# Two PSUM accumulators with alternating sums, and tensor-by-scalar products on GpSimd, in a convolution and feed-forward kernel

## The chip, the core and the metric

The kernel runs on one core of a Trainium2 chip. The metric is the device time of one execution in microseconds (us), lower being better. Three executions of the kernel before took 510.12, 510.33 and 511.39 us (median 510.33).

The engines are called as the profile calls them: PE (TensorE) multiplies matrices and writes its results into PSUM, DVE (VectorE), ACT (ScalarE) and POOL (GpSimd) work on tiles, and SP (SyncE) sends DMAs. POOL sends DMAs too.

## The reference

```python
# x: (8, 3904, 192), weight: (8 heads, 7 taps); 8 heads of 24 channels
w = softmax(weight, axis=-1)
x_pad = np.concatenate([np.zeros((B, 6, D)), x], axis=1)
out[b, s, h*24:(h+1)*24] = sum over k of w[h, k] * x_pad[b, s + k, h*24:(h+1)*24]
x = out.reshape(31232, 192)
a = x @ w1                      # 192 x 1024
b = x @ w2                      # 192 x 1024
return ((a * b) @ w3) @ w_out   # 1024 x 1024, 1024 x 192
```

A causal convolution of 7 taps, one set of taps to each head, goes along each of the 8 sequences of 3904 rows. Its output goes into two products with 192 x 1024 weights, the elementwise product of the two follows, and then the two weights at the end, which the kernel multiplies into one of 1024 x 192 (`W_sb`) beforehand.

## The kernel before, in words

**Rows and rounds.** The 31232 rows are halved into two streams of 15616 (`NS = 2`, index r). A round R is 512 consecutive rows of both streams (`CH = 512`); there are 31, the last one with 256 rows. The channels go in three pieces of 64 (`NP = 3`, index k); a tile of 128 partitions holds one such piece of both streams.

**First product** (`first_product`, L618 to L651). For each round and each of the eight 128-column blocks ft of the weights, PE makes `pa` (with w1) and `pb` (with w2), six matmuls of 512 columns each, three channel pieces by two streams, the two streams on the two halves of the array's rows. ACT copies `pa` to `asb` in bf16 (L640), and DVE multiplies `asb` by `pb` into `abT` (L643). `pa` and `pb` take one PSUM quarter each.

**Second product** (`second_product`, L678 to L703; `half_rows` in four later phases). For a round and a stream, PE multiplies `abT` by `W_sb` into one quarter `ops` in 32 matmuls of 192 columns, ACT copies it to `osb` (L690), and SP sends it out.

**Quarters.** All of PSUM is four buffers of 128 x 2 x 512 fp32 (two banks each), one pool tag that is handed round in turn (`banks`, L104). Whatever PE writes takes the next of the four, and waits until the last reader of what was in it is done.

**Phases.** Three rounds at a time make a phase p, counted from 0: the first products of its rounds (24 steps of `pa` and `pb`), then the second products of the same rounds (six, one for each round and stream). In phases 0, 2 and 5 matmuls of the convolution stand between the second products (`places`, `convolve`). The fourth and fifth phase are p = 3 and p = 4, and hold none.

**Where the convolution is done.** For most rows by PE, as products with a band matrix. For the rounds in `SIDE` it is done elsewhere, by *tasks*: one channel piece of two rounds each. Rows are cast to bf16 in HBM by DMAs of the POOL queue (`side_cast`, L506), transposed into a `raw` tile by DMAs of the SP queue (`side_transpose`, L515), ACT makes the first of seven terms into an fp32 accumulator (`side_first`, L520), and DVE adds the six others, one SCALAR_TENSOR_TENSOR each: raw x tap + accumulator (`side_sums`, L538). The last of them writes bf16 into `side`, which a later phase's first products read. There are two accumulators in SBUF, `acc_of[0]` and `acc_of[1]`, taken in turn by tasks. A planner (L797 to L816) fills phases with sums by a room of 12 sums a phase, so two whole tasks, one after the other, in p = 3 (tasks 5 and 6) and in p = 4 (tasks 7 and 8). `side_steps` (L821) issues them between the second products: an entry with a number (`at`) is a task's first term on ACT, due after so many second products; sums follow in the list's order up to the next first term that isn't issued yet.

**What POOL does beside this.** Half tasks (`POOL_AT`), 512 rows each, by a product into `tmp` (L584, TENSOR_TENSOR with a tap broadcast over the row) and an addition (L596, last one L591). In phases 3 to 6 POOL has two half tasks each, issued at the start of the first products, and behind them a one-element copy `pace` (L948) that holds the DMAs of the POOL queue until a given step of the first products is done.

Of the kernel before, what the change touches and what calls it, by code (L numbers as in the profile page):

```python
# [8 lines left out]
FP32 = mybir.dt.float32  # L9
BF16 = mybir.dt.bfloat16  # L10
AX = mybir.AxisListType
ALU = mybir.AluOpType
# [4 lines left out]
def kernel(  # L17
# [10 lines left out]
    nc = tc.nc  # L28

    B, S, D = x.shape  # L30
    H, K = weight.shape
# [5 lines left out]
    NS = 2  # L37
    TS = B * S // NS
    CH = 512
# [34 lines left out]
    t0 = (LAG + 3) * CH  # L74
# [25 lines left out]
    psum = ctx.enter_context(tc.tile_pool(name="psum", bufs=4, space=bass.MemoryType.PSUM))  # L100
    dram = ctx.enter_context(tc.tile_pool(name="dram", bufs=1, space=bass.MemoryType.DRAM))
    ctx.enter_context(tc.manual_schedule())

    def banks(name):  # L104
        return psum.tile([128, NS, CH], FP32, tag="banks", name=name)

    def banks_bf16(name):
        return psum.tile([128, 16, 128], BF16, tag="banks", name=name)

    def slot(shape, dtype, name):  # L110
        return stage.tile(shape, dtype, tag="slot", bufs=6, name=name)
# [76 lines left out]
    for r in range(NS):  # L188
        p = group(r, 0).start
# [12 lines left out]
        out=diag, in_=diag, pattern=[[-1, 128 + 8]], compare_op=ALU.is_equal,  # L202
# [11 lines left out]
    for i in range(4):  # L214
        d = diag[i * C:i * C + C, i * C + 2 * i:i * C + 2 * i + C]
        nc.vector.tensor_copy(
            out=cmask[i * C:i * C + C],
# [62 lines left out]
    for i in range(4):  # L280
# [16 lines left out]
        op=ALU.mult)  # L297
    for r, w0, w1, f in ((0, 0, HW, A), (1, HW // 2, HW, A), (1, 0, HW // 2, V)):
        f(out=xb_of[0][0][0][group(r, 0), w0:w1, :], in_=begin[group(r, 0), w0:w1, :])
    p = group(1, 0).start  # L300
# [177 lines left out]
    for q in SIDE:  # L478
        for k in range(NP):
            left = [h for h in range(2) if (q, k, h) not in BY_POOL]  # L480
            if left:
                tasks.append((q, k, half_of(q, left[0])[0], half_of(q, left[-1])[1]))
    side_of, acc_of, raw_of, cast_to = {}, [], [], set()
    RAW = HALO + 2 * CH

    def side_tiles():
# [31 lines left out]
    def side_first(i):  # L518
        p, k, t0, t1 = tasks[i]
        nc.scalar.activation(  # L520
            out=acc_of[i % 2][:, 0:t1 - t0], in_=raw_of[i % 5 - 1][:, HALO - 1:HALO - 1 + t1 - t0],
            func=ACT.Copy, scale=wC[:, k, K - 2:K - 1])

    def side_sums(i):
        p, k, t0, t1 = tasks[i]
        starts = [z for z in range(0, TS, S) if t0 <= z < t1]
        o = t0 - side_span(p)[0]

        def job(d, last):
            def run():  # L530
                raw, acc = raw_of[i % 5 - 1], acc_of[i % 2]
                if d == 2:
                    for z in starts:
                        nc.vector.memset(acc[:, z - t0:z - t0 + 1], 0.0)
                for lo, hi in [(t0, t1)] if last else \
                        zip([t0] + [z + d for z in starts], starts + [t1]):
                    a = acc[:, lo - t0:hi - t0]
                    nc.vector.scalar_tensor_tensor(  # L538
                        out=side_of[p][:, k, o:o + t1 - t0] if last else a,
                        in0=raw[:, HALO + lo - t0 - d:HALO + hi - t0 - d],  # L540
                        scalar=wC[:, k, K - 1 - d:K - d], in1=a, op0=ALU.mult, op1=ALU.add)
            return run
        size = (t1 - t0) / (2 * CH)
        return [(size, job(d, d == 0)) for d in list(range(2, K)) + [0]]
# [30 lines left out]
    def pool_sums(lane, own, p, k, half):  # L575
        _, _, t0, starts = pool_half(p, k, half)

        def job(d):
            def run():
                acc, tmp = pool_acc[lane], pool_tmp  # L580
                if d == 2:
                    for z in starts:
                        nc.gpsimd.memset(acc[:, z - t0:z - t0 + 1], 0.0)
                nc.gpsimd.tensor_tensor(  # L584
                    out=acc if d == 1 else tmp, in0=pool_raw[lane][:, HALO - d:HALO - d + CH],
                    in1=wC[:, k, K - 1 - d:K - d].to_broadcast([128, CH]), op=ALU.mult)
                if d == 1:
                    return
                if d == 0:
                    o = half * CH  # L590
                    nc.gpsimd.tensor_tensor(out=side_of[p][:, k, o:o + CH], in0=acc, in1=tmp,  # L591
                                            op=ALU.add)
                    return
                for lo, hi in zip([t0] + [z + d for z in starts], starts + [t0 + CH]):
                    a = acc[:, lo - t0:hi - t0]
                    nc.gpsimd.tensor_tensor(out=a, in0=a, in1=tmp[:, lo - t0:hi - t0],  # L596
                                            op=ALU.add)
            return run
        return [job(d) for d in list(range(1 if own else 2, K)) + [0]]
# [202 lines left out]
    for i, cost, f in steps:  # L802
        while room < cost:
            p += 1
            room = rooms[p]
            at, ends = 0, {}
            starts.setdefault(p, [])
        if i not in begun:
            begun.add(i)
            starts[p].append(i)  # L810
            n = max(p == 0, int(at) // 2 - 1, -(-ends.get(i - 2, 0) // 2))
            chain.setdefault(p, []).append((i, n, lambda i=i: side_first(i), 0))
        assert p < stage_of(2 * tasks[i][0] + 1)
        room, at = room - cost, at + cost
        chain.setdefault(p, []).append((i, None, f, cost))
        ends[i] = at  # L816
    for p in starts:
        for i in starts[p]:
            assert i < 5 or p < 2 or max(v for v in chain if chain[v][0][0] <= i - 5) <= p - 1
# [109 lines left out]
    for p, (rounds, ends) in enumerate(phases):  # L929
        todo = jobs.pop(p, [])  # L930

        last = len(points) - 1
        lanes = pool_sum.pop(p, ())
        counts = [0] * 7 if len(lanes) > 1 else [0] * 3 + [2] * 4 if p == 1 else [2] * 2 + [1] * 5
        at = [[todo.pop(0) for _ in range(min(n, len(todo)))] for n in counts + [len(todo)]]
        if p in places:
            at[last - 1].insert(0, clear)
        elif len(lanes) > 1:
            at[last].insert(0, clear)
        for fs in lanes:  # L940
            for v, f in enumerate(fs):
                at[v if len(lanes) == 1 else 0].append(f)
        if p == 3:
            part_tile()

        def issue(R, ft, fs):
            def run():
                P(out=pace, in_=abT_of[R][0:1, ft, 1, 0:2] if ft else asb_of[0][0:1, 1, 0:2])  # L948
                for f in fs:
                    f()  # L950
            return run

        for j, R in enumerate(rounds):
            first_product(R, {ft: issue(R, ft, at[v])
                              for v, (a, ft) in enumerate(((0, 0),) + points[1:] if
                                                          len(lanes) > 1 else points)
                              if a == j and at[v]})
        assert not todo
        if len(lanes) < 2:
            clear()  # L960
        if p == 0:
            pool_tiles()
        turn(p)
        raws = starts.get(p + 1, ())
        late = [i for i in raws if p == 0 or len(lanes) > 1 or i >= 5 and chain[p][0][0] <= i - 5]
        if p > 1:
            for lane, t in enumerate(pool_from.get(p, ())):
                pool_transpose(lane, *t)
        for i in raws:
            if i not in late:  # L970
                side_transpose(i)
        if p == 1:
            pool_transpose(0, *pool_from[p][0])
        state = set()
        side_steps(p, 0, state)
        for n, (R, r) in enumerate((R, r) for R in ends for r in range(NS)):
            halves = p in (6, 7, 8, 9)
            if halves and r == 0:
                opss = [banks("ops") for _ in range(NS)]
                mms = [half_rows(R, i, opss[i], 0) for i in range(NS)]  # L980
                relays = [passed(mm) for mm in mms]
                for i in range(NS):
                    half_rows(R, i, opss[i], 1, relays[i])
            if (R, r) == (NR - 1, NS - 1):
                last_product(R, r)
            else:
                second_product(R, r, results if p == 0 else None, opss[r] if halves else None)
            if n == 4 and len(pool_from.get(p, ())) > 1:
                for lane, t in enumerate(pool_from[p]):
                    pool_first(lane, *t)  # L990
            if n in places.get(p, ()):
                convolve(p)
            side_steps(p, n + 1, state)
        assert len(state) == len(chain.get(p, ()))
        while results:
            results.pop(0)()
        for b, js in rest:
            store(b, js=js)
        rest.clear()
        for i in late:  # L1000
            side_transpose(i)
        turn(p)
# [31 lines left out]
```

## Time and profile before

| | |
|---|---|
| median of 3 runs | 510.33 us (510.12 to 511.39) |
| the profiled execution, its own time | 510.0 us |
| its span, first to last instruction | 508.3 us |
| what lies around the span | 1.7 us |
| fourth phase (p = 3), first product from | 166.16 us |
| fourth phase, second product from | 197.35 us |
| fifth phase (p = 4), first product from | 213.30 us |
| fifth phase, second product from | 244.49 us |
| sixth phase (p = 5) from | 260.43 us |

Times inside an execution are counted from the start of the span. A row of a timeline gives the start, the length, the engine, the line, the operation with its tiles (out<-in), how many instructions it merges, and in brackets the idle time before it and what ended that. A row of the windows gives a stretch, its length, each engine's busy time with the number of instructions, TensorE's granted clock, the DMA share and GB/s. PEld is PE's weight load, which overlaps its matmuls. POOLq and SPq are DMA queues.

### The profile page before, as it was taken

The numbers are of one execution on the slowest core, as the hardware profiler recorded it, in microseconds if no ns is written. First come the engines' busy times: TensorE is split into PE (matmuls) and PEld (weight loads), VectorE is DVE, ScalarE is ACT, GpSimd is POOL, SyncE is SP. The second block draws the span as 40 slices with busy tenths as digits, with TensorE's granted clock in tenths as the row PEclk, the third lists the DMA queues.
The fourth block names the chain that finished last, engine by engine and source line by source line (L and its number), as shares of the span: only waits on it lengthen the run. The fifth ranks groups of instructions, "written<-read, shape, count | busy, mean of one in ns | idle before, by whom it ended". The sixth has DMA issues, their size and how long they took to land.

```text
span 508.3 us, 14981 instructions
## 1 busy us (share of the span) xinstructions
PE 502.7 (99%) x6372; PEld 336.7 (66%) x6372; DVE 446.1 (88%) x402; ACT 349.0 (69%) x390; POOL 255.9 (50%) x340
## 2 busy tenths in 40 slices
PE   8999999999999999999999999999999999999997
PEld 4546865595569557845874596569457855975697
DVE  7898769999999799999999998999999999999930
ACT  6786667746779776577567778763776477457742
POOL 9975201332890799499879944992371056000000
PEclk9999999999999999999999999999999999999999
DMA  9999979999969868990999097619402500240025
GB/s 138 158 172 164 164 150 182 148 165 185 164 41 167 150 144 102 215 139 13 91 235 110 4 162 147 124 29 183 111 1 61 171 2 1 65 126 1 2 64 156
DMA packets 161118, 58.54 MB, mean 115 GB/s; under 512 B 116895, under 2 KB 161051, under 8 KB 161051
## 3 DMA queue, kind: packets, MB, share of 16 engines
q1 hardware_dynamic: 85963, 40.02, 38.0%
q0 software_dynamic: 74784, 17.37, 37.4%
q8 instruction: 50, 0.82, 0.7%
q10 hardware_dynamic: 304, 0.20, 0.1%
q14 instruction: 17, 0.14, 0.1%
HBM read 35.02 MB, written 34.85 MB: 137 GB/s over the span
## 4 chain that ended last, share of the span: by engine, by line
PE 97%; DMA 1%; ACT 0%; POOL 0%; DVE 0%; issue 0%; POOLq 0%
PE pa L633 31%; PE pb L633 31%; PE ops L685 21%; PE ops L664 10%; PE cps L345 1%; PE wps L758 1%; DMA xb<-in_x_dram 1%; PE tps L420 0%; PE ops L711 0%; DVE abT L643 0%; PE tps L435 0%; PE cps L375 0%; ACT asb L640 0%; POOL xb L165 0%; ACT convo L355 0%
## 5 line engine op out<-in xcount | busy, mean ns | idle before, releaser
L643 DVE TENSOR_TENSOR abT<-asb,pb 128x1024 bf16<-128x1024 bf16 x240 | 292.6, 1220 | 28.7 <-ACT asb L640 12.7
L640 ACT CAST asb<-pa 128x1024 bf16<-128x1024 f32 x244 | 247.0, 1012 | 64.0 <-PE pa L633 63.8
L633 PEld LDWEIGHTS <-wn 64*128 64x128 bf16 x1488 | 138.8, 94 | 81.1 <-issue 0.9
L633 PEld LDWEIGHTS <-ws 64*128 64x128 bf16 x1488 | 130.3, 94 | 70.4 <-issue 0.9
L685 PE MATMUL ops<-W_sb,abT 128*128 128x192 bf16 x1296 | 110.0, 246 | 0.0
L685 PEld LDWEIGHTS <-abT 128*128 128x128 bf16 x1296 | 106.0, 98 | 4.6 <-issue 4.6
L690 ACT COPY osb<-ops 128x768 f32<-128x768 f32 (+1 forms) x61 | 48.4, 794 | 82.3 <-PE ops L685 47.0
L633 PE MATMUL pb<-xT,wn 64*128 64x512 bf16 x376 | 103.6, 376 | 0.0
L633 PE MATMUL pa<-xT,ws 64*128 64x512 bf16 x376 | 103.5, 376 | 0.0
L633 PE MATMUL pa<-xT,wn 64*128 64x512 bf16 x376 | 102.9, 376 | 0.1
L633 PE MATMUL pb<-xT,ws 64*128 64x512 bf16 x376 | 102.2, 376 | 0.0
L633 PE MATMUL pb<-side,wn 64*128 64x512 bf16 (+1 forms) x368 | 100.5, 369 | 0.0
L633 PE MATMUL pa<-side,ws 64*128 64x512 bf16 (+1 forms) x368 | 99.3, 369 | 0.0
L633 PE MATMUL pa<-side,wn 64*128 64x512 bf16 (+1 forms) x368 | 99.3, 369 | 0.0
L633 PE MATMUL pb<-side,ws 64*128 64x512 bf16 (+1 forms) x368 | 98.1, 369 | 0.0
L538 DVE SCALAR_TENSOR_TENSOR acc<-raw,wC,acc 128x1024 f32<-128x1024 bf16 (+2 forms) x70 | 84.5, 1208 | 2.1
L596 POOL TENSOR_TENSOR acc<-acc,tmp 128x512 f32<-128x512 f32 (+6 forms) x60 | 70.3, 1176 | 4.3
L584 POOL TENSOR_TENSOR tmp<-acc,wC 128x512 f32<-128x512 bf16 x66 | 68.5, 1038 | 3.5
L948 POOL COPY pace<-abT 1x2 bf16<-1x2 bf16 x28 | 4.9, 174 | 110.3 <-DVE abT L643 110.2
L664 PEld LDWEIGHTS <-abT 64*128 64x128 bf16 x1280 | 53.0, 94 | 0.9
L664 PE MATMUL ops<-W_sb,abT 64*128 64x192 bf16 x1280 | 53.5, 243 | 0.0
L506 POOL DMA_DIRECT2D rows_c<-in_x_dram x58 | 40.6, 706 | 6.5 <-DMA rows_c<-in_x_dram 2.8
(85 smaller groups left out, 245.1 us busy)
## 6 DMA issues: line engine op xcount, KB each, us to landing
out_dram<-osb SPq DMA_DIRECT2D x54, 384.0 KB
xb<-in_x_dram POOLq DMA_DIRECT2D x16, 240.0 KB, 7.5
out_dram<-osb SPq DMA_DIRECT2D x12, 192.0 KB
rows_c<-in_x_dram POOLq DMA_DIRECT2D x14, 130.0 KB, 7.5
rows_c<-in_x_dram POOLq DMA_DIRECT2D x14, 128.0 KB, 5.9
xb<-in_x_dram POOLq DMA_DIRECT2D x6, 228.0 KB, 11.7
w3b<-in_moe_w_dram POOLq DMA_DIRECT2D x4, 256.0 KB, 5.4
w3b<-in_moe_w_dram POOLq DMA_DIRECT2D x8, 128.0 KB, 4.7
```

The lines of the kernel that those rows point to most:

```text
L345: nc.tensor.matmul(o.rearrange("p (w g) -> p w g", g=wd)[:, :, c - c0:c1 - c0], Aband[group(r, e), h, :], xb[group(r, e), s:s + m, c:c1], ...
L506: nc.gpsimd.dma_start(out=rows_c[lo:t1, k, r * Q:r * Q + Q], in_=x_rows[r * TS + lo:r * TS + t1, k * Q:k * Q + Q])
L538: nc.vector.scalar_tensor_tensor(out=side_of[p][:, k, o:o + t1 - t0] if last else a, in0=raw[:, HALO + lo - t0 - d:HALO + hi - t0 - d], sc ...
L584: nc.gpsimd.tensor_tensor(out=acc if d == 1 else tmp, in0=pool_raw[lane][:, HALO - d:HALO - d + CH], in1=wC[:, k, K - 1 - d:K - d].to_broa ...
L596: nc.gpsimd.tensor_tensor(out=a, in0=a, in1=tmp[:, lo - t0:hi - t0], op=ALU.add)
L633: nc.tensor.matmul(p[:, r, f * N:f * N + N], w_of(i, k, r)[rs, ft * 128:(ft + 1) * 128], operand(R, k, rs), start=(k == 0), stop=(k == NP ...
L640: nc.scalar.copy(out=asb[:, :, 0:per * N], in_=pa[:, :, 0:per * N])
L643: nc.vector.tensor_tensor(out=ab[:, f0, :, 0:N], in0=asb[:, :, 0:N], in1=pb[:, :, 0:N], op=ALU.mult)
L664: mm = nc.tensor.matmul(ops[:, a, g * D:g * D + D], ab[rs, jt, r, q * 128:(q + 1) * 128], W_sb[rs, jt, :], start=(turn == 0 and g == 0 and ...
L685: nc.tensor.matmul(ops[:, g // 2, (g % 2) * D:(g % 2) * D + D], ab[:, jt, r, g * 128:(g + 1) * 128], W_sb[:, jt, :], start=(jt == 0), stop ...
L690: nc.scalar.copy(out=osb.rearrange("p (a g) d -> p a (g d)", g=2), in_=ops[:, 0:ng // 2, 0:2 * D])
L758: nc.tensor.matmul(wps[:, q, 0:D], w3T[:, g, q, :, :, t].rearrange("p j b -> p (j b)"), wo_b[:, g, t, :], start=(g + t == 0), stop=(g == G ...
```

## The change

Three things are changed.

First, the four PSUM quarters are allocated once, as four tiles in a list, and `banks` hands them round in turn by rotating the list. What was one pool tag with four buffers is now four tiles whose uses are ordered by what reads and writes them.

Second, in p = 3 and p = 4 the third and fourth quarter of the list (those that the last `pa` and `pb` of the first products have used) are taken out before the second products and become the accumulators of the phase's two tasks. The second products go round in the two that are left. Behind them the two go back into the list, as second and fourth. Both first terms are issued by ACT ahead of the first second product, and the sums of the two tasks alternate: one of the one, one of the other, twelve in all.

Third, POOL's products are TENSOR_SCALAR with the tap as a scalar per partition, in all phases that have them. Additions stay.

On DVE, the program of both kernels has 24 multiplications, 12 sums, 24 multiplications, 12 sums in p = 3 and p = 4; only the order within the twelve and where the accumulator lies differ. On PE, POOL and SP the instructions stand in the same order as before. On ACT only the two first terms of p = 3 and p = 4 have moved.

```diff
+    quarters = [psum.tile([128, NS, CH], FP32, tag=f"q{i}", bufs=1, name="quarter")
+                for i in range(4)]
+
     def banks(name):
-        return psum.tile([128, NS, CH], FP32, tag="banks", name=name)
+        quarters.append(quarters.pop(0))
+        return quarters[-1]
 
     def banks_bf16(name):
-        return psum.tile([128, 16, 128], BF16, tag="banks", name=name)
+        return banks(name).rearrange("p a c -> p (a c)").bitcast(BF16).rearrange(
+            "p (w c) -> p w c", c=128)
...
+    in_psum = {}
+
+    def acc_at(i):
+        return in_psum[i] if i in in_psum else acc_of[i % 2]
...
     def side_first(i):
         p, k, t0, t1 = tasks[i]
         nc.scalar.activation(
-            out=acc_of[i % 2][:, 0:t1 - t0], in_=raw_of[i % 5 - 1][:, HALO - 1:HALO - 1 + t1 - t0],
+            out=acc_at(i)[:, 0:t1 - t0], in_=raw_of[i % 5 - 1][:, HALO - 1:HALO - 1 + t1 - t0],
             func=ACT.Copy, scale=wC[:, k, K - 2:K - 1])
...
-                raw, acc = raw_of[i % 5 - 1], acc_of[i % 2]
+                raw, acc = raw_of[i % 5 - 1], acc_at(i)
...
-                nc.gpsimd.tensor_tensor(
+                nc.gpsimd.tensor_scalar(
                     out=acc if d == 1 else tmp, in0=pool_raw[lane][:, HALO - d:HALO - d + CH],
-                    in1=wC[:, k, K - 1 - d:K - d].to_broadcast([128, CH]), op=ALU.mult)
+                    scalar1=wC[:, k, K - 1 - d:K - d], scalar2=None, op0=ALU.mult)
...
+    for p in (3, 4):
+        firsts = [(i, 0, f, c) for i, at, f, c in chain[p] if at is not None]
+        sums = [[v for v in chain[p] if v[0] == i and v[1] is None] for i in starts[p]]
+        assert len(firsts) == 2 and all(len(v) == K - 1 for v in sums)
+        chain[p] = firsts + [v for pair in zip(*sums) for v in pair]
...
-        state = set()
+        state, held = set(), []
+        if p in (3, 4):
+            for i in starts[p]:
+                held.append(quarters.pop(2))
+                in_psum[i] = held[-1].rearrange("p a c -> p (a c)")
         side_steps(p, 0, state)
...
         assert len(state) == len(chain.get(p, ()))
+        for i, q in enumerate(held):
+            quarters.insert(2 * i + 1, q)
```

## Prediction

> **What bounds the kernel now.** I read the page first, then the windows by stage, the chain of waits through the stages that change, and the timelines of DVE and ACT there. The page gives each engine's busy time, and the chain that ended last by engine:
>
> ```profile
> PE 502.7 (99%) x6372; PEld 336.7 (66%) x6372; DVE 446.1 (88%) x402; ACT 349.0 (69%) x390; POOL 255.9 (50%) x340
> PE 97%; DMA 1%; ACT 0%; POOL 0%; DVE 0%; issue 0%; POOLq 0%
> ```
>
> PE is busy 502.7 of 508.3 us, so all its idle time is 5.6 us, and the chain is PE. A busy share is an average, so the windows come next: fourth phase (first product, second product), fifth phase (the same), and the last 28 us.
>
> ```profile
> 166.16:197.35 31.19, 31.19 (x290) 15.55 (x290) 27.71 (x23) 24.64 (x25) 27.45 (x25) 1.00 0.64 130
> 197.35:213.30 15.95, 15.95 (x195) 15.79 (x196) 15.54 (x13) 7.72 (x10) 10.43 (x18) 1.00 1.51 171
> 213.30:244.49 31.19, 31.19 (x289) 15.29 (x290) 29.01 (x24) 24.65 (x25) 27.88 (x32) 1.00 0.54 83
> 244.49:260.43 15.94, 15.94 (x194) 15.78 (x196) 15.54 (x13) 7.72 (x10) 11.64 (x19) 1.00 1.40 167
> 480.00:508.30 28.30, 24.84 (x394) 24.02 (x390) 7.75 (x8) 10.66 (x14) 0.00 (x0) 1.00 0.32 99
> ```
>
> PE fills each of the four stages to the last hundredth, at a granted clock of 1.00. DVE is nearly as full (15.54 of 15.95 us in the second products), which is what makes the change look useful. But full beside full says nothing about who waits. Busy could also hide a PE that is held back, so I look at the pace in the chain, in order of time, over the border of the two phases:
>
> ```profile
> 213.30 0.75 PE pa L633 x6
> 214.05 0.65 PE pb L633 x6
> 214.70 0.65 PE pa L633 x6
> 215.35 0.65 PE pb L633 x6
> 216.00 0.65 PE pa L633 x6
> 216.64 0.65 PE pb L633 x6
> ...
> 244.49 15.95 PE ops L685 x192
> ```
>
> Six matmuls take 0.65 us from the second group on, whether DVE is late or not, and the groups follow each other without a hole: 24 steps of 2 x 0.65 are the 31.19 us of the stage. The second products are 192 matmuls in 15.95 us, 83 ns each. No piece of another engine stands between them. PE goes at its own pace here, and a DVE or POOL that is faster can't shorten these 94.27 us.
>
> So the one question is whether the change makes PE wait. For that I need when DVE is done with its sums. Its timeline at the end of the fourth phase and at the end of the fifth:
>
> ```profile
> 197.79 1.22 DVE L643 TENSOR_TENSOR abT<-asb,pb 128x1024 bf16<-128x1024 bf16 x1
> ```
>
> ```profile
> 198.93 6.56 DVE L538 SCALAR_TENSOR_TENSOR acc<-side,wC,acc 128x1024 f32<-128x1024 bf16 x5
> 205.52 1.28 DVE L538 SCALAR_TENSOR_TENSOR side<-side,wC,acc 128x1024 bf16<-128x1024 bf16 x1
> 206.72 6.56 DVE L538 SCALAR_TENSOR_TENSOR acc<-raw,wC,acc 128x1024 f32<-128x1024 bf16 x5
> 213.32 1.28 DVE L538 SCALAR_TENSOR_TENSOR side<-raw,wC,acc 128x1024 bf16<-128x1024 bf16 x1
> 215.14 3.81 DVE L643 TENSOR_TENSOR abT<-asb,pb 128x1024 bf16<-128x1024 bf16 x3 [0.53 <-ACT asb L640]
> ...
> 246.06 6.56 DVE L538 SCALAR_TENSOR_TENSOR acc<-raw,wC,acc 128x1024 f32<-128x1024 bf16 x5
> ...
> 262.27 2.52 DVE L643 TENSOR_TENSOR abT<-asb,pb 128x1024 bf16<-128x1024 bf16 x2 [0.53 <-ACT asb L640]
> ```
>
> The sums end at 213.32 + 1.28 = 214.60 us, and the next multiplication starts at 215.14, held by ACT's `asb` and not by DVE: 0.53 us of slack already, in both phases.
>
> **The change, part by part.**
>
> *Alternating the sums.* Starts of dependent sums lie (205.52 - 198.93) / 5 = 1.32 us apart: each starts about 0.03 us after the one before has ended (1.28). Where one task follows another, 206.72 - 205.52 = 1.20 us: an independent sum starts before the other has ended. So twelve sums now take 10 x 1.32 + 1.20 + 1.28 = 15.68 us; alternating at 1.20 they would take 11 x 1.20 + 1.28 = 14.48 us, 1.2 us less in each of the two phases. DVE would be done at 213.4 instead of 214.6 and wait 1.7 instead of 0.53 us for `asb`. Late next is the same ACT copy behind the same `pa`. Worth on the path: 0.
>
> *The accumulator in PSUM.* No DVE instruction of this trace writes PSUM, so I bound it. The rows by form:
>
> ```profile
> L643 DVE TENSOR_TENSOR abT<-asb,pb 128x1024 bf16<-128x1024 bf16 x240 | 292.6, 1220 | 28.7 <-ACT asb L640 12.7 <-PE cps L345 0.3
> L538 DVE SCALAR_TENSOR_TENSOR acc<-raw,wC,acc 128x1024 f32<-128x1024 bf16 x55 | 70.6, 1284 | 1.7
> L538 DVE SCALAR_TENSOR_TENSOR acc<-raw,wC,acc 128x512 f32<-128x512 bf16 x5 | 3.8, 751 | 0.1
> ```
>
> A sum costs (1284 - 751) / 512 = 1.041 ns per element, so 218 ns of 1284 are fixed. A multiplication that reads PSUM has 1220 - 1066 = 154 ns fixed: reading PSUM shows no extra cost. From below, a start 198.93 - 197.79 = 1.14 us after an independent instruction has been seen. From above, I let the fixed part double for the write and let nothing overlap: 1.28 + 0.22 + 0.03 = 1.53 us. I take 1.20, since it is the same instruction without a dependence, and keep 1.14 to 1.53.
>
> The Trainium skill speaks against this part: "Perfetto Trace Analysis", section "Optimizing Scalar/DVE Operations", gives a fixed cost per DVE instruction of about 60 ns on SBUF and 125 ns on PSUM. By it, as an estimate, a sum would start every 1.27 us instead of 1.20, or every 1.39 if dependence counted as well. The one row here that touches PSUM, the multiplication, does not show it for reads, and none shows a write.
>
> *What PE now waits for.* Held out of the round, the third and fourth quarter come back as second and fourth, so the next phase goes: first `pa` into a free one, first `pb` into the first accumulator, second `pa` into a free one, second `pb` into the other. The first `pb` (214.05) must wait for the eleventh sum, the second (215.35) for the twelfth. With sums starting every s us and lasting s + 0.08 (1.28 against 1.20), the eleventh ends at 198.93 + 11 s + 0.08, and with some 0.04 us to hand over it must be there by 214.01: s = 1.364. The twelfth has the same bound within a hundredth, by way of the multiplication behind it, which must free its `pb` by 216.64. At s = 1.20 PE has 1.8 us to spare, and at today's dependent pace of 1.32 still 0.5. In the fifth phase the sums start at 246.06 and the first `pb` is due 0.75 us after 260.43, which gives 1.37. Cost: 0.
>
> *Only two quarters for six second products.* ACT's timeline in the fourth phase:
>
> ```profile
> 197.65 1.15 ACT L520 ACTIVATE acc<-side,wC 128x1024 f32<-128x1024 bf16 x1
> 200.13 0.80 ACT L690 COPY osb<-ops 128x768 f32<-128x768 f32 x1 [1.33 <-PE ops L685]
> 202.78 0.80 ACT L690 COPY osb<-ops 128x768 f32<-128x768 f32 x1 [1.84 <-PE ops L685]
> 203.47 1.15 ACT L520 ACTIVATE acc<-raw,wC 128x1024 f32<-128x1024 bf16 x1
> ...
> 213.34 0.80 ACT L690 COPY osb<-ops 128x768 f32<-128x768 f32 x1 [0.61 <-PE ops L685]
> 214.09 1.01 ACT L640 CAST asb<-pa 128x1024 bf16<-128x1024 f32 x1
> ```
>
> One second product takes 15.95 / 6 = 2.66 us. The third needs the first one's quarter at 197.35 + 2 x 2.66 = 202.67, and the copy that frees it ends at 200.93: 1.7 us of cover, and the later ones have the same. The second first term moves from 203.47 to the front. It waits for the last multiplication (its quarter was the last `pb`), which ends at 199.01, and runs until 200.17. Queued behind it on ACT is the copy of the first second product, 0.04 us later than before, with 1.7 us of cover. The second sum wants this term at 198.93 + 1.20 = 200.13, so DVE loses some 0.1 us once. At the end, the second `pa` needs the quarter of the sixth second product: copied by 214.14, needed at 214.70, 0.56 us of cover. Without this cover ACT's lateness would be PE's, one for one. Cost: 0. `raw` of the second task is wanted 4.5 us earlier; its transposes come from the phase before.
>
> *GpSimd's products.* The nearest rows on POOL:
>
> ```profile
> L584 POOL TENSOR_TENSOR tmp<-acc,wC 128x512 f32<-128x512 bf16 x66 | 68.5, 1038 | 3.5
> L596 POOL TENSOR_TENSOR acc<-acc,tmp 128x512 f32<-128x512 f32 x50 | 63.3, 1267 | 3.9
> L227 POOL COPY ws<-wn 64x256 bf16<-64x256 bf16 x12 | 4.6, 396 | 0.5
> L227 POOL COPY ws<-wn 64x128 bf16<-64x128 bf16 x6 | 1.6, 290 | 0.2
> ```
>
> A one-input copy goes by (396 - 290) / 128 = 0.83 ns per element, so 396 + 256 x 0.83 = 0.61 us for 512. The upper end is a two-input addition, 1.27 us. I take 0.7, nearer to the copy, as the new form has one tensor input: twelve of them save 4 us of POOL in a phase with two half tasks, or cost 2.8 at the upper end. Behind them stands the `pace` copy and then the queue's DMAs:
>
> ```profile
> 197.78 0.17 POOL L948 COPY pace<-abT 1x2 bf16<-1x2 bf16 x1
> 198.27 5.44 POOL L506 DMA_DIRECT2D rows_c<-in_x_dram  x8 [0.32 <-issue]
> ```
>
> By the code this `pace` reads what the last multiplication but one wrote, and that has ended when the last begins (197.79). So a faster POOL idles ahead of it and the DMAs start when they did. Slower, they start up to 2.8 us later, and what they bring goes by transposes into `raw` tiles read from 246.06 on, over 40 us later. Cost: 0.
>
> *Quarters as four fixed tiles.* PE's and POOL's order is unchanged; some of PE's waits on its own earlier writes into the same quarter go, mostly in the first 25 us, each a wait on something three quarters back. Bounds: 0 and a few tenths gained; I take 0.
>
> **Sum.** 510.0 us for the profiled execution, plus 0 in the fourth and the fifth phase, plus 0 elsewhere: 510.0. The executions shown are 510.0, 510.12, 510.33 and 511.39, the profiled one 0.33 below the median of the other three. I put the middle of the four: 510.2.
>
> **Rivals.**
>
> 1. *The sums don't get faster* (PSUM costs what alternating saves, s of 1.3 or a little above): the change doesn't do what it says, and below 1.364 PE doesn't notice, up to 1.43 hardly. Time 510.2. For it: the unmeasured write. Chance 0.22, all of it within 0.3%.
>
> 2. *The accumulators hold PE's quarters too long* (slower). The place is the first `pb` of the fifth and of the sixth phase, the price 11 to 12 us of PE wait for every us by which s exceeds 1.364, in two phases. At s = 1.43 that is 1.6 us, 511.8; at the upper bound 1.53 it is 12 x 0.166 x 2 = 4.0 us, 514.2. For it: the slack is thin per sum (0.16 us), and before the change none of the four quarters was held by DVE's sums. Against it: it needs more than the dependent pace, with the dependence gone. Chance of s above 1.43: 0.09.
>
> 3. *POOL gets slower and its DMAs late*: decides only if a product cost over 1.5 us, beyond all rows shown. Some 512. Chance 0.02.
>
> 4. *PE's 5.6 us of idle time shrink*: 3.46 of them are in the last 28 us (28.30 - 24.84), after all that is changed, so only the waits of the start are left; 1.6 us or more is hardly there. 508.6. Chance 0.03.
>
> **How the numbers follow.** A measurement of this kernel tells about 0.3% (1.5 us) from no change. The forecast (shorter sums, nothing waits) has 0.64, with rival 1 it is 0.86 for the same time; faster 0.03, slower 0.11. The likeliest's own range is 509.4 to 511.2, from the spread of the executions and a few tenths at the start; the upper end is stretched to 512.0 for the near part of rival 2.
>
> **What would show it.** Right: in the profile after, PE again fills both phases, 47.1 us from the first `pa` to the next phase's; the sums start every 1.20 to 1.27 us; the first multiplication behind them waits over 1 us for `asb`; POOL's products are under 0.9 us and its `pace` waits for DVE. Wrong: a wait of PE's `pb` for a DVE sum at the two borders, or sums longer than 1.36 us apart; a copy of `ops` that PE waits for; or a start shorter by over a microsecond.

## The result, and the profile after

The changed kernel took 527.22 us (median of 6 runs, 526.46 to 531.14) where the kernel before took 510.03 (6 runs): a ratio of 1.035, interval [1.031, 1.039]. It is slower by some 17 us. The forecast was 510.2, and 527 lies far outside its range.

The profiled execution took 527.43 us with a span of 525.4, 17.1 us more than the span before. From the page of the changed kernel: busy time by engine, the chain that ended last by engine, and the group of POOL's products.

```profile
PE 505.7 (96%) x6372; PEld 343.0 (65%) x6372; DVE 450.1 (86%) x402; ACT 349.1 (66%) x390; POOL 299.8 (57%) x340
PE 76%; POOL 15%; DMA 5%; issue 2%; ACT 1%; DVE 1%; POOLq 0%; ACTq 0%; DVEq 0%
L594 POOL TENSOR_SCALAR tmp<-acc,wC 128x512 f32<-128x512 bf16 x66 | 106.6, 1615 | 4.6
```

POOL has 44 us more work (299.8 against 255.9), and 38 of them are this one group: 66 products of 1.615 us where they were 1.038. The chain, which was 97% PE, is now 76% PE, 15% POOL and 5% DMA. PE's own work is 3.0 us longer, and its idle time went from 5.6 to 19.7 us.

Where? The windows of five phases, the fourth to the eighth, each from its first `pa` to that of the next. Before, the fourth is 31.19 + 15.95 = 47.14 and the fifth 47.13 us by the rows in the prediction; the three that follow are the first fence, and the second fence is all five after. Columns as in the prediction.

```profile
260.43:308.95 48.52, 48.52 (x579) 31.41 (x580) 45.79 (x37) 37.95 (x43) 34.43 (x37) 1.00 0.86 117
308.95:355.95 47.00, 47.00 (x674) 31.22 (x676) 43.21 (x36) 30.12 (x31) 33.30 (x34) 1.00 0.72 115
355.95:402.95 47.00, 47.00 (x677) 31.37 (x673) 44.43 (x40) 31.39 (x34) 15.77 (x20) 1.00 0.29 76
```

```profile
166.30:213.50 47.20, 47.20 (x483) 32.34 (x484) 43.69 (x37) 32.52 (x34) 41.13 (x36) 1.00 0.79 147
213.50:263.80 50.30, 47.38 (x481) 32.23 (x480) 43.42 (x37) 32.38 (x34) 43.75 (x47) 1.00 0.64 89
263.80:323.37 59.57, 50.12 (x580) 32.81 (x580) 44.82 (x35) 37.85 (x43) 48.48 (x44) 0.94 0.75 101
323.37:371.70 48.33, 47.20 (x675) 32.66 (x676) 46.24 (x37) 30.13 (x31) 43.84 (x36) 1.00 0.81 127
371.70:420.26 48.56, 47.09 (x675) 32.84 (x672) 46.28 (x41) 31.38 (x33) 19.54 (x20) 1.00 0.42 83
```

The fourth phase is unchanged. The four after it lost 3.2, 11.1, 1.3 and 1.6 us, together 17.1, which is all of it. PE's idle time (length minus its busy time) is 2.92 + 9.45 + 1.13 + 1.47 = 15.0 us of that; the other 2.1 us are PE being busy for longer, 1.6 of them in the sixth phase, where the granted clock was 0.94.

What PE waited for is in the view of the waits of the changed kernel (engine, line, what it waited for: us in total, times, longest), and one step back ACT's wait:

```profile
ACT asb L650 <- POOL pace L963: 14.6, 3, 10.6
...
PE quarter L643 <- ACT asb L650: 11.9, 2, 9.4
...
PE quarter L643 <- DVE abT L653: 3.0, 3, 1.5
```

PE never waits for a DVE sum, the danger that the prediction priced. Four fifths of the wait shown is for ACT's copy into `asb`, which waits for POOL's one-element copy `pace`; the remaining 3.0 us are for DVE's multiplications. The kernel's code tells why: the first `pace` of a phase (`ft` is 0, L963) reads `asb`, not `abT`, and `asb` has three buffers (L649), so the fourth copy of the phase may not be written until POOL has read the first. POOL's timeline before, at the first border (from the fourth phase to the fifth) and at the second (from the fifth to the sixth), shows how much room there was:

```profile
215.24 0.17 POOL L948 COPY pace<-asb 1x2 bf16<-1x2 bf16 x1 [1.54 <-ACT asb L640]
...
245.45 0.18 POOL L948 COPY pace<-abT 1x2 bf16<-1x2 bf16 x1
...
261.82 0.52 POOL L165 DMA_DIRECT2D xb<-in_x_dram  x1 [1.11 <-DMA rows_c<-in_x_dram]
262.38 0.17 POOL L948 COPY pace<-asb 1x2 bf16<-1x2 bf16 x1
```

At the first border POOL was early by 1.54 us; at the second it came straight from issuing DMAs, with no idle time at all. ACT's fourth copy then started 2.6 us after `pace` had ended, at both borders (timeline of ACT before):

```profile
218.02 1.01 ACT L640 CAST asb<-pa 128x1024 bf16<-128x1024 f32 x1 [0.33 <-PE pa L633]
...
265.16 1.01 ACT L640 CAST asb<-pa 128x1024 bf16<-128x1024 f32 x1 [0.33 <-PE pa L633]
```

And after, POOL's timeline and ACT's:

```profile
204.46 0.17 POOL L963 COPY pace<-abT 1x2 bf16<-1x2 bf16 x1
...
221.31 0.17 POOL L963 COPY pace<-asb 1x2 bf16<-1x2 bf16 x1
...
258.11 0.17 POOL L963 COPY pace<-abT 1x2 bf16<-1x2 bf16 x1
...
278.68 0.18 POOL L963 COPY pace<-asb 1x2 bf16<-1x2 bf16 x1
```

```profile
221.52 2.93 ACT L650 CAST asb<-quarter 128x1024 bf16<-128x1024 f32 x3 [3.61 <-POOL pace L963]
...
278.89 1.93 ACT L650 CAST asb<-quarter 128x1024 bf16<-128x1024 f32 x2 [10.57 <-POOL pace L963]
```

Follow the lateness. Twelve products of 1.56 instead of 1.04 us are 6.3 us in a phase. The `pace` on `abT` ends the products of the fourth phase at 204.46 instead of 197.78, 6.7 us late. Behind it the DMAs are issued, then the `pace` on `asb`: 221.31 instead of 215.24, 6.1 us late, of which 2.6 were free. ACT starts its copy within 0.05 us of POOL's release. Another 6.3 us are added in the fifth phase: 258.11 instead of 245.45 is 12.7 us late, and the DMAs behind it take 3.6 us longer, so the next release is at 278.68 instead of 262.38, 16.3 us late. Of these 2.6 were free and 3.4 are PE's own lateness by then, which leaves 10.3; ACT's 10.57 counts the 0.28 us that lie between two copies anyway. In the chain of the changed kernel the longest piece ahead of this release is one of those DMAs (start, length):

```profile
262.72 13.13 DMA rows_c<-in_x_dram
```

Why the DMAs take longer when they are issued later is not shown by any run.

The sums, meanwhile, did what was forecast (timeline of DVE after):

```profile
211.14 1.28 DVE L548 SCALAR_TENSOR_TENSOR side<-side,wC,quarter 128x1024 bf16<-128x1024 bf16 x1
212.33 1.28 DVE L548 SCALAR_TENSOR_TENSOR side<-raw,wC,quarter 128x1024 bf16<-128x1024 bf16 x1
215.35 3.84 DVE L653 TENSOR_TENSOR abT<-asb,quarter 128x1024 bf16<-128x1024 bf16 x3 [1.74 <-ACT asb L650]
```

They start 1.19 us apart and DVE is done 1.74 us before it is wanted.

### The profile page after: what moved, and what is told of

Same layout as the page of the kernel before. It is cut to its first block, busy times and chain, and to the rows that moved or that the text cites. A ratio compares the mean times of both kernels' runs of the same rounds, so it can differ in the third digit from the quotient of the medians.

```text
span 525.4 us, 14989 instructions
## 1 busy us (share of the span) xinstructions
PE 505.7 (96%) x6372; PEld 343.0 (65%) x6372; DVE 450.1 (86%) x402; ACT 349.1 (66%) x390; POOL 299.8 (57%) x340
## 4 chain that ended last, share of the span: by engine, by line
PE 76%; POOL 15%; DMA 5%; issue 2%; ACT 1%; DVE 1%; POOLq 0%; ACTq 0%; DVEq 0%
PE quarter L643 47%; PE quarter L695 15%; PE quarter L674 10%; POOL tmp L594 7%; POOL acc L606 5%; DMA rows_c<-in_x_dram 5%; POOL rows_c L516 2%; PE quarter L350 1%; PE quarter L768 1%; PE quarter L251 1%; POOL side L601 1%; ACT asb L650 1%; DVE abT L653 1%; POOL xb L170 0%; PE quarter L425 0%
## 5 line engine op out<-in xcount | busy, mean ns | idle before, releaser
L653 DVE TENSOR_TENSOR abT<-asb,quarter 128x1024 bf16<-128x1024 bf16 x240 | 292.0, 1221 | 43.2 <-ACT asb L650 28.0
L650 ACT CAST asb<-quarter 128x1024 bf16<-128x1024 f32 x244 | 246.8, 1012 | 81.6 <-PE quarter L643 66.8
L643 PE MATMUL quarter<-xT,wn 64*128 64x512 bf16 x752 | 176.4, 378 | 9.6 <-ACT asb L650 9.4
L643 PE MATMUL quarter<-xT,ws 64*128 64x512 bf16 x752 | 177.4, 378 | 0.0
L643 PE MATMUL quarter<-side,wn 64*128 64x512 bf16 (+1 forms) x736 | 165.8, 369 | 5.5 <-DVE abT L653 3.0
L643 PE MATMUL quarter<-side,ws 64*128 64x512 bf16 (+1 forms) x736 | 165.6, 369 | 0.0
L695 PE MATMUL quarter<-W_sb,abT 128*128 128x192 bf16 x1296 | 110.0, 246 | 0.0
L594 POOL TENSOR_SCALAR tmp<-acc,wC 128x512 f32<-128x512 bf16 x66 | 106.6, 1615 | 4.6
L700 ACT COPY osb<-quarter 128x768 f32<-128x768 f32 (+1 forms) x61 | 48.5, 794 | 81.7 <-PE quarter L695 46.4
L963 POOL COPY pace<-abT 1x2 bf16<-1x2 bf16 x28 | 9.0, 320 | 95.3 <-DVE abT L653 95.3
L674 PE MATMUL quarter<-W_sb,abT 64*128 64x192 bf16 x1280 | 53.5, 243 | 0.0
```

The lines of the kernel that those rows point to most:

```text
L594: nc.gpsimd.tensor_scalar(out=acc if d == 1 else tmp, in0=pool_raw[lane][:, HALO - d:HALO - d + CH], scalar1=wC[:, k, K - 1 - d:K - d], sc ...
L643: nc.tensor.matmul(p[:, r, f * N:f * N + N], w_of(i, k, r)[rs, ft * 128:(ft + 1) * 128], operand(R, k, rs), start=(k == 0), stop=(k == NP ...
L650: nc.scalar.copy(out=asb[:, :, 0:per * N], in_=pa[:, :, 0:per * N])
L653: nc.vector.tensor_tensor(out=ab[:, f0, :, 0:N], in0=asb[:, :, 0:N], in1=pb[:, :, 0:N], op=ALU.mult)
L674: mm = nc.tensor.matmul(ops[:, a, g * D:g * D + D], ab[rs, jt, r, q * 128:(q + 1) * 128], W_sb[rs, jt, :], start=(turn == 0 and g == 0 and ...
L695: nc.tensor.matmul(ops[:, g // 2, (g % 2) * D:(g % 2) * D + D], ab[:, jt, r, g * 128:(g + 1) * 128], W_sb[:, jt, :], start=(jt == 0), stop ...
```

## The experiments

The first theory (A): POOL's products got dearer, and the delay reaches PE by way of `pace` and `asb`. The rival (B): the two quarters held as accumulators, or PSUM itself, hold up PE or DVE. Diffs are against the changed kernel if nothing else is said. Times are medians beside the kernel before on the same chip (509.65 to 510.09 us); four of the kernels ran only once, so they have no interval.

**1. The changed kernel, with POOL's products as before.**

```diff
-nc.gpsimd.tensor_scalar(..., scalar1=wC[:, k, K - 1 - d:K - d], scalar2=None, op0=ALU.mult)
+nc.gpsimd.tensor_tensor(..., in1=wC[:, k, K - 1 - d:K - d].to_broadcast([128, CH]), op=ALU.mult)
```

> The changed kernel with POOL's products as TENSOR_TENSOR again; quarters, PSUM accumulators and alternating sums stay. Theory A (the whole loss is POOL's slower product, which makes POOL late for the copy that reads asb, so that ACT may not write asb again and PE stops): 510.0 us, within 0.3% of the kernel before, no wait of ACT for POOL, sums every 1.19 us. Theory B (the accumulators that hold two quarters cost it): 520 to 527.

Measured: 510.40 us, ratio 1.0008 [0.9999, 1.0017]. DVE's timeline at the first border, and POOL's at both:

```profile
215.35 31.01 DVE L653 TENSOR_TENSOR abT<-asb,quarter 128x1024 bf16<-128x1024 bf16 x24 [1.75 <-ACT asb L650]
```

```profile
215.45 0.17 POOL L963 COPY pace<-asb 1x2 bf16<-1x2 bf16 x1 [4.74 <-ACT asb L650]
...
262.59 0.17 POOL L963 COPY pace<-asb 1x2 bf16<-1x2 bf16 x1 [1.19 <-ACT asb L650]
```

POOL is early by 4.74 and 1.19 us, and ACT never waits for it. With the same products the kernel before showed 1.54 and 0 us: what POOL's DMAs leave free differs between these two traces. All of the loss goes with the products; rival B falls. The PSUM accumulators and the alternation cost nothing that can be measured and bring nothing, though DVE now waits 1.75 us.

**2. The kernel before, with the new products alone** (the same two lines, the other way round).

> The kernel before with POOL's products as TENSOR_SCALAR; accumulators in SBUF, sums one task after the other. Theory A: at least the 527 of the changed kernel, 527 to 533: the same waits of ACT for POOL's copy (about 14 us in all), and on top DVE's sums in the fourth and fifth phase slow down where they lie beside POOL's products (2.0 to 2.3 us instead of 1.28). Theory B: 510.

Measured: 536.95 us, ratio 1.053 [1.050, 1.055]. The products alone cost more than the whole change, and more than the 527 to 533 expected. From the view of DVE's sums by line: count, then shortest, median and longest in ns; first the kernel before, then this one.

```profile
L538 DVE SCALAR_TENSOR_TENSOR acc<-raw,wC,acc x70: 747/1284/1286, 102.8 to 449.1; 128x1024 f32<-128x1024 bf16 x55, 128x768 f32<-128x768 bf16 x10, 128x512 f32<-128x512 bf16 x5
```

```profile
L538 DVE SCALAR_TENSOR_TENSOR acc<-raw,wC,acc x70: 746/1285/2314, 102.6 to 475.2; 128x1024 f32<-128x1024 bf16 x55, 128x768 f32<-128x768 bf16 x10, 128x512 f32<-128x512 bf16 x5
```

With POOL late, its work lies beside the sums, and sums of 1.28 us take up to 2.31. The expectation had named this, but put the whole cost too low. ACT waited 21.5 us for `pace` here, against 14.6 after the whole change.

**3. The first `pace` of a phase reads `abT`, not `asb`.** If `asb` is the only thing that POOL's lateness holds, most of the loss should go.

```diff
-P(out=pace, in_=abT_of[R][0:1, ft, 1, 0:2] if ft else asb_of[0][0:1, 1, 0:2])
+P(out=pace, in_=abT_of[R][0:1, ft, 1, 0:2])
```

> The changed kernel, but POOL's first one-element copy of a phase reads abT of that step instead of asb, so that a late POOL no longer holds an asb buffer. Theory A: faster than the changed kernel by 3 us or more; back to 510 if the hold on asb is all that a late POOL does, but about 516 to 524 if the wait moves to the next thing POOL owes (ACT's first term of POOL's next half tasks, which needs POOL's accumulators), since POOL's work in the fifth phase is 57 us from copy to copy and PE's is 47. Theory B: unchanged, 527.

Measured: 530.56 us, ratio 1.040 [1.038, 1.041]: no faster than the changed kernel, so this expectation failed. ACT's wait for `pace` is gone, and another stands in its place (timeline of ACT):

```profile
325.18 0.72 ACT L581 ACTIVATE acc<-acc,wC 128x512 f32<-128x512 bf16 x1 [13.26 <-DMA acc<-rows_c]
325.81 0.78 ACT L700 COPY osb<-quarter 128x768 f32<-128x768 f32 x1
```

ACT's first term of POOL's next half task waits 13.3 us for its rows. A DMA of the SP queue brings them into the buffer that POOL's products still read, so it starts only when the last product has ended (chain of this run, start and length):

```profile
321.02 1.57 POOL tmp L594
322.61 2.49 DMA acc<-rows_c
```

Behind the first term on ACT stands the copy that empties a quarter, and PE waits 11.8 us for that. Six products of this phase took 2.41 us beside DVE's sums, so POOL was later here than by the new form alone. Still, `asb` was the first reader to feel it and not the cause: POOL's round of products, additions and DMAs no longer fits into a phase, and whoever waits for POOL first stops PE.

**4. Accumulators back in SBUF, alternation and new products kept** (the block that takes the two quarters out is removed).

```diff
-if p in (3, 4):
-    for i in starts[p]:
-        held.append(quarters.pop(2))
-        in_psum[i] = held[-1].rearrange("p a c -> p (a c)")
```

> The changed kernel with the two accumulators in SBUF: sums alternate, POOL's products stay TENSOR_SCALAR, no quarter is held. Theory A: not faster than the changed kernel, 527 to 532: POOL's waits stay, and DVE's sums beside POOL's products take 2 us or more where they took 1.28 in PSUM. Theory B: 510 to 515, since no quarter is held.

Measured: 537.40 us, ratio 1.053 [1.049, 1.056], beyond the expected 527 to 532. Without any quarter held the loss is larger, so PSUM accumulators *saved* some 10 us once POOL was late. DVE's timeline and POOL's, at the same place:

```profile
200.04 1.28 DVE L548 SCALAR_TENSOR_TENSOR acc<-side,wC,acc 128x1024 f32<-128x1024 bf16 x1
201.24 2.29 DVE L548 SCALAR_TENSOR_TENSOR acc<-raw,wC,acc 128x1024 f32<-128x1024 bf16 x1
...
205.08 2.30 DVE L548 SCALAR_TENSOR_TENSOR acc<-raw,wC,acc 128x1024 f32<-128x1024 bf16 x1
207.31 1.27 DVE L548 SCALAR_TENSOR_TENSOR acc<-side,wC,acc 128x1024 f32<-128x1024 bf16 x1
```

```profile
201.12 1.32 POOL L606 TENSOR_TENSOR acc<-acc,tmp 128x512 f32<-128x512 f32 x1
202.54 2.41 POOL L594 TENSOR_SCALAR tmp<-acc,wC 128x512 f32<-128x512 bf16 x1
...
206.25 1.18 POOL L963 COPY pace<-abT 1x2 bf16<-1x2 bf16 x1
```

Sums beside POOL's work are long (the first, beside the end of a product, is not), and 1.27 us from 207.31 on, where POOL has turned to DMAs. POOL suffers too: a product of 2.41 us, a one-element copy of 1.18 instead of 0.17.

**5. The new product in the second half task of a phase only**, half the dose. If the cost is in proportion, half of 17 us should appear; if there is a threshold, far less.

```diff
+if lane == 1:
     nc.gpsimd.tensor_scalar(..., scalar1=wC[:, k, K - 1 - d:K - d], scalar2=None, op0=ALU.mult)
+else:
+    nc.gpsimd.tensor_tensor(..., in1=wC[:, k, K - 1 - d:K - d].to_broadcast([128, CH]), op=ALU.mult)
```

> The changed kernel with TENSOR_SCALAR only in the second of two half tasks of a phase, TENSOR_TENSOR in the first (half the dose). Theory A with a threshold (POOL has little to spare from phase to phase, and only what exceeds it is paid): 6 x 0.52 = 3.1 us more POOL work a phase. In the fifth phase the copy comes at about 216.8 and is needed by 218, no stop; in the sixth at about 267 and is needed by 265.1, so PE stops some 2 us, and DVE's sums beside POOL's products cost 1 us more: 513, between 511 and 515. Without a threshold, in proportion to the dose, it would be 518.5.

Measured: 512.72 us, ratio 1.0053 [1.0036, 1.0070]. One wait, at the second border (waits, then POOL's timeline):

```profile
ACT asb L655 <- POOL pace L968: 1.9, 1, 1.9
```

```profile
216.55 0.17 POOL L968 COPY pace<-asb 1x2 bf16<-1x2 bf16 x1 [0.91 <-ACT asb L655]
...
267.87 0.17 POOL L968 COPY pace<-asb 1x2 bf16<-1x2 bf16 x1
```

A threshold it is: 2.6 us for half the dose, as expected. At the first border POOL still came 0.91 us early, so no lateness was carried over, and the stop comes from the fifth phase alone. From the first of these two copies to the second POOL took 51.32 us, where it took 47.14 in experiment 1: 4.2 us more, of which 2.6 are free ahead of ACT's fourth copy. That leaves 1.6, and ACT's 1.9 counts the 0.3 us that lie between two copies anyway. Six dearer products are 3.1 us of the 4.2; the 1.19 us of idle time were used up, and the rest, some 2 us, is that the DMAs behind the products took longer.

**6. A constant in place of the tap** (the half tasks' taps are left out, the form of the instruction stays).

```diff
-scalar1=wC[:, k, K - 1 - d:K - d]
+scalar1=0.25
```

> The changed kernel with POOL's TENSOR_SCALAR multiplying by a constant 0.25 instead of the tap that it reads per partition (left out: the taps of POOL's half tasks). If the slow part is the reading of a scalar per partition: products of 0.6 to 0.8 us and 510. If it is the operation itself: products of 1.56 us and 527.

Measured: 523.11 us, ratio 1.025 [1.023, 1.027]. From the view of the line, in ns as above:

```profile
L594 POOL TENSOR_SCALAR tmp<-acc x66: 1478/1488/2344, 128.1 to 445.7; 128x512 f32<-128x512 bf16 x66
```

Products are 1.49 us, nearer to the second case of the expectation: reading the scalar from a tile makes 0.07 us of the 0.52. The rest belongs to the form.

**7. Alternation in SBUF, products as before** (4 and 1 together; one execution).

> Alternating sums with accumulators in SBUF and POOL's TENSOR_TENSOR. If alternating alone brings DVE's pace: sums start every 1.20 us, twelve take 14.5 us, time 510 since PE does not wait for DVE there. If the PSUM accumulator brings it: 1.28 us or more from start to start.

Measured: 510.61 us. The sums start 1.20 us apart (198.94, 200.14, ... 212.10), and DVE then waits 1.84 us for `asb`. The order alone brings the whole gain in pace; PSUM adds nothing to it.

**8. PSUM, but one task after the other, products as before** (one execution).

```diff
-chain[p] = firsts + [v for pair in zip(*sums) for v in pair]
+chain[p] = firsts + sums[0] + sums[1]
```

> Accumulators in PSUM, but one task's sums after the other's, POOL's TENSOR_TENSOR. If PSUM costs nothing more than SBUF when a sum depends on the one before: 1.32 us from start to start, 510. If a dependent write and read of PSUM takes longer: 1.37 us or more, and PE would wait for the accumulators at the two borders, 510.5 to 514.

Measured: 511.45 us; about 1.05 us of what it has more was there before the fourth phase's second products began, ahead of what was changed. DVE's timeline:

```profile
199.99 6.59 DVE L548 SCALAR_TENSOR_TENSOR quarter<-side,wC,quarter 128x1024 f32<-128x1024 bf16 x5
206.61 1.28 DVE L548 SCALAR_TENSOR_TENSOR side<-side,wC,quarter 128x1024 bf16<-128x1024 bf16 x1
207.81 6.58 DVE L548 SCALAR_TENSOR_TENSOR quarter<-raw,wC,quarter 128x1024 f32<-128x1024 bf16 x5
```

Dependent sums are (206.61 - 199.99) / 5 = 1.324 us apart, independent ones 1.20: in PSUM the same two figures as in SBUF.

**9. Each product as two of 256 columns** (one execution).

```diff
+for c0 in (0, CH // 2):
+    nc.gpsimd.tensor_scalar(out=(...)[:, c0:c0 + CH // 2], in0=pool_raw[lane][:, HALO - d + c0:HALO - d + c0 + CH // 2], ...)
```

> The changed kernel with each TENSOR_SCALAR product of POOL as two of 256 columns. It gives the fixed part and the part per element of that operation, which the one 512-column row can't. If it is mostly per element: about 0.85 us each, so 1.7 us a product, POOL a little later still, 529 to 533. If it is mostly fixed: 1.2 us or more each, and well over 535.

Measured: 546.31 us, far beyond the 529 to 533 that the expectation had for this price. In ns by line:

```profile
L595 POOL TENSOR_SCALAR tmp<-acc,wC x132: 912/922/1985, 129.0 to 467.6; 128x256 f32<-128x256 bf16 x132
```

256 columns take 0.92 us and 512 take 1.56: 2.5 ns per element and some 0.28 us fixed. The new form is slow per element. A copy in the trace of before goes at 0.83 ns per element.

**10. Products into a bf16 `tmp`** (one execution; the products are rounded to bf16 before the addition).

```diff
-acc, tmp = pool_acc[lane], pool_tmp
+acc, tmp = pool_acc[lane], pool_tmp.bitcast(BF16)[:, 0:CH]
```

> The changed kernel with POOL's products written in bf16 into tmp instead of fp32 (the first product of the single half tasks stays fp32; the products are rounded). If TENSOR_SCALAR is slow because it turns bf16 into fp32: products of about 1 us and about 510 to 515. If the type doesn't matter: 1.5 to 1.6 us and 527.

Measured: 526.61 us, the median product 1.565 us. The type of the output does not matter. The additions behind it fall from 1.27 to 1.16 us, at most 1.3 us in a phase, too little to change the picture.

No version beats the kernel before. The best of them, 1 and 7, equal it, since PE fills both phases there by itself.

## Why the prediction was wrong, point by point

- **PE at its own pace: right.** With the products as before (experiment 1), 1.2 us less of sums in each of two phases changes the time by a ratio of 1.0008, not told from 1.
- **Alternating the sums: right.** 1.20 us from start to start forecast, 1.19 measured; DVE waits 1.74 us for `asb`, forecast 1.7.
- **The accumulator in PSUM: right.** 1.20 us taken, 1.19 measured, the dependent pace 1.324 against 1.32 in SBUF. The Trainium skill's rule in "Perfetto Trace Analysis", section "Optimizing Scalar/DVE Operations", which would have made it 1.27 or 1.39, is not borne out: on this DVE instruction the traces show no added cost for PSUM.
- **What PE waits for, and two quarters for six second products: right.** PE waited for no sum, and neither border cost anything in experiment 1.
- **The quarters as fixed tiles: right**, the span of experiment 1 is 508.4 us against 508.3.
- **GpSimd's products: this step failed, twice.** First the price: "I take 0.7, nearer to the copy, as the new form has one tensor input", with bounds of 0.61 and 1.27. It is 1.56, outside both. The number of tensor inputs was no guide: each row used as a bound was an instruction of another kind, and that the new kind might be slower than all of them was excluded without a reason. Second, who waits: the step looked at the `pace` behind the products and at what its DMAs bring "over 40 us later", and wrote "Cost: 0". The next thing on POOL's queue is the *first* `pace` of the next phase, which reads `asb`. By the trace of before ACT waits for that after 1.54 + 2.61 = 4.15 us of lateness at the first border, and at the second, where POOL had no idle time, after 2.6, with what the first border left over on top. If the DMAs in between took no longer, 24 products dearer by 4.15 us in all would reach ACT there: 1.04 + 4.15 / 24 = 1.21 us each, *below* the step's own upper bound of 1.27. By the idle times of experiment 1 the fifth phase alone decides, with 1.19 + 2.6 us free: 1.04 + 3.8 / 12 = 1.36 us, above the bound. So whether the step was free by its own prices isn't settled; at 1.56 us it was not, by either.
- **Rival 3 named the cause** ("POOL gets slower and its DMAs late", beyond 1.5 us) with a chance of 0.02 and "Some 512". Its time was too small since it stopped at the DMAs; the place was the buffer that POOL's reading holds, and the lateness grows from phase to phase.
- **What no step had: POOL and DVE disturb each other.** In the kernel before POOL was done before the sums began. Once late, it lay beside them. In the changed kernel the sixth and seventh phase have their accumulators in SBUF, and at the start of the seventh and of the eighth PE waits 1.1 and 1.5 us for DVE, which comes late from such sums: five in a row took 10.04 us from 307.62 on, where five took 6.56 before.

How much of the 17 us each mechanism would cost alone is not settled. Shown are the idle times above and that they vanish with the products' form. That longer sums made POOL later in experiments 2 and 4, and so the stops longer, is what their timelines suggest, and it is not separated. Nor is it known why the DMAs behind the products took longer, 3.6 us of the second stop. A fourth `asb` buffer wasn't tried. Why this form takes 2.5 ns per element on POOL stays open; the scalar's read (0.07 us) and the output's type (none) are not it, and an input of another type wasn't tried.

## What to carry to other kernels

Before an instruction on a side engine is given another form, ask for the price of that very form at that size; where no row has it, rows of other operations don't bound it, and what is wanted is the price from which it hurts. For that, follow the engine's queue round a whole period, sum what a period adds against its idle time, and look at *every* instruction that its next steps release, small pacing copies above all, since a copy that reads a buffer holds it. An engine that is 50% busy over the whole span can be full in the phases that count.

## What the runs showed of the hardware

**A tensor-by-scalar product on POOL is slower than a tensor by a broadcast tensor**: 1.56 us against 1.04 for 128 x 512, bf16 to fp32, with 2.5 ns per element. The Trainium skill, "GPSIMD Engine Reference", section "Engine selection", says that one-input operations of this engine run roughly at line rate; for this form the measurement differs (the copy of one input has 0.83 ns per element).

**DVE's sums and POOL's work disturb each other in SBUF, not in PSUM.** Sums by line in the changed kernel, in ns (`acc` lies in SBUF, `quarter` in PSUM):

```profile
L548 DVE SCALAR_TENSOR_TENSOR acc<-raw,wC,acc x55: 746/1285/2307, 102.9 to 466.4; 128x1024 f32<-128x1024 bf16 x40, 128x768 f32<-128x768 bf16 x10, 128x512 f32<-128x512 bf16 x5
...
L548 DVE SCALAR_TENSOR_TENSOR quarter<-raw,wC,quarter x15: 1280/1282/1290, 200.4 to 260.4; 128x1024 f32<-128x1024 bf16 x15
```

POOL's products and additions of the fifth phase ran until 258.11, beside the sums in PSUM from 249.56 on, and none of these is over 1.29 us, nor are POOL's products longer than 1.56. In SBUF the sums reach 2.31. The Trainium skill's rule agrees with that: "SBUF — State Buffer", section "Who interferes with whom", says that a DVE instruction with two SBUF inputs contends with a GpSimd instruction that reads SBUF, and one with at most one SBUF input does not.

**The clock falls in a long stop of PE.** Windows of the changed kernel through the second stop, in which PE did nothing from 270.50 to 279.95 (the clock stands behind POOL's column):

```profile
275.00:276.00 1.00, 0.00 (x0) 0.00 (x0) 0.00 (x0) 0.00 (x0) 0.00 (x0) 0.91 1.41 119
276.00:277.00 1.00, 0.00 (x0) 0.00 (x0) 0.00 (x0) 0.00 (x0) 0.69 (x1) 0.50 3.27 106
...
282.00:283.00 1.00, 1.00 (x9) 0.47 (x7) 0.48 (x2) 0.47 (x1) 1.00 (x1) 0.67 1.50 206
283.00:284.00 1.00, 1.00 (x12) 0.54 (x10) 1.00 (x1) 0.58 (x1) 0.92 (x2) 1.00 1.53 134
```

It went to half some 5.3 us after PE's last work and came back some 2.7 us after the restart, so PE worked at half speed for 2.7 us and lost about 1.4, most of the 1.6 us of longer busy time in that phase. PE's stop of 2.9 us in the fifth phase left the clock at 1.00. The Trainium skill, "TensorE: Matmul & The Clock Gate", section "What's actually happening", gives an idle window of about 3.4 us before the clock is halved and a busy one of the same length before it returns; the two stops do not contradict the first, as 2.9 us is shorter and the clock fell 5.3 us into the longer one, and the return, at 2.7 us, was somewhat quicker.
